# Output steps token tile by token tile, two product banks that swap by group, and QKV weights without a gap, in a fused attention and feed-forward kernel

## The chip, the cores and the metric

The kernel runs on one core of a Trainium2 chip. The metric is device time in microseconds, the median of the timed runs. The engines are PE (TensorE: matmuls, PEld its weight loads), ACT (ScalarE), DVE (VectorE), POOL (GpSimd) and SP (SyncE, which issues most DMAs). Each works through its own instructions in the order in which the program gives them out.

## What is computed

The input `x` has 2048 tokens of width 576. The result is the input, plus a local attention, plus a feed-forward layer with ReLU, both on the normalised input.

```
xn  = layernorm(x)
q, k, v = split(xn @ wqkv)            # 32 heads of width 18
logits[s, w] = q[s] . k[s - 2 w] / sqrt(18),   w = 0 .. 7   (no key before token 0)
a   = softmax(logits) @ v[s - 2 w]
out = x + a @ wo + max(xn @ w1, 0) @ w2        # w1: 576 x 4608, w2: 4608 x 576
```

## The kernel before

All matmuls run in a reduced-precision fp32 form. Each operand is kept as a high part (a rounded copy, made by ACT) and a low part (the difference, made by DVE), and each product is the sum of three: high by high, high by low, low by high. `hi_lo` makes such a pair.

The tokens are treated in two passes (`ph`) of 1024 each, eight tiles of 128 tokens. The 4608 hidden columns are treated in 18 steps `n` of 256 columns. A **group** `g` is one step `n` for one half `h` of the pass, 512 tokens; there are 72 groups. `m = g // 2` counts the weight sets; set `m` lies in `BUF[m % 2]`, as eight slots (T1, B11, T2, B21, T3, B22, T4, RR) in a high and a low half.

**First products** (`xn @ w1`) of a group make four hidden tiles of 256 columns of tokens (`j` = 0, 1) by 128 hidden columns (`f` = 0, 1). From the third weight set on they use a Strassen-Winograd form with seven products, P1 to P7, in `pstep`. Each is six matmuls (`terms`), or eight with the remaining 64 rows (`rest`). They accumulate in three PSUM banks, `bk2`, `bkA` and `bk3`; partial sums are copied to `bkA` (after P1), SN5 (after P5) and SN2 (after P6). `h_parts` applies the ReLU and makes the high part (`hhi`, ACT) and the low part (`hlo`, DVE) of a hidden tile. The tile (j, f) = (0, 0) comes out of P2, (1, 1) out of P7 by an addition into SN5, (0, 1) out of P3 by an addition into SN2, and (1, 0) out of P4 directly from the bank. In the trace, P-steps are the PE rows `bk<-xs`, `bk<-xa` and `bkA<-xa` with `bk<-xr` or `bkA<-xr` for the remaining rows; the additions are `sn<-bk,sn`.

**Second products** (`h @ w2`) of group `g - 1` are spread between the seven products of group `g`. An output step (`o_step(g, j, idx, k)`) is six matmuls for one hidden tile (`idx`) and one token tile of 128 (`k` = 0, 1; rows `po<-w2t`). Token tile `k` accumulates in the bank pair `po[k]`. After the last step of a token tile, ACT copies the sum out (`x<-po`) and writes the next token tile's running sum into the bank (`po<-x`, the seed). `items` lists the hidden tiles of a group and, in some groups, attention output times `wo` (`("wo", u)`, for four groups `u` of heads, and `("wo", NU)` for what is left). `o_list` gives the order of the output steps.

**Attention.** Eight times, QKV tiles (`qkv_tile`, rows `pm<-wset,xa`) are computed between the products of two groups; their weights (`wq_make`, view `wqset`) lie in the buffer that the next weight set will use, and are loaded as its slots come free. The attention proper is a list of long DVE operations (`later`), taken up when DVE has nothing more urgent. Its output is turned through DRAM (`turned`) and loaded by `wo_h`.

**Order.** The whole program is put in order by hand. The class `Order` keeps a clock per engine from estimated durations. Each small ACT or DVE operation has a slack, which becomes its due time; among those that are ready, the earliest due goes first. `force` gives out whatever a PE step needs before it. `tick` counts the steps of a group, and `plan` (`at(g, idx, f)`) hangs other work on a tick: weight preparation (`set_make`; `fine` after a QKV stage, when parts are made one by one), `w2_make`, `wo_make`, `wo_h`, and copies of weights to a packed form in DRAM (`w1_keep`, `w2_keep`, `wq_keep`, `wo_keep`), which POOL issues. The order of a group before:

```
steps = ("P5", 0), ("P1", 0), ("P6", 0), ("P2", None), ("P7", 1), ("P3", 1), ("P4", None)
cnt = {"P5": l0 // 3, "P1": l0 - l0 // 3 - l0 // 4, "P6": l0 // 4, "P7": l1 // 2, "P3": l1 - l1 // 2}
```

The second entry is the `j` whose output steps follow; with four steps for each `j` these are one after P5, two after P1, one after P6, two after P7 and two after P3.

## Time and profile before

| | |
|---|---|
| median of three timed runs | 1185.26 us (1184.56 to 1187.47) |
| profiled execution | 1186.34 us |
| its span, first to last instruction | 1184.6 us |
| mean granted TensorE clock | 0.997 |
| PE busy | 1142.5 us, 8528 matmuls |
| PE weight loads busy | 1115.6 us |
| DVE busy | 824.2 us |
| ACT busy | 742.4 us |
| DMA | 115.60 MB, 98 GB/s |

In the rows of the profile, a line of the kernel is often that of a helper: L284 is every matmul, L278 every ACT copy, L281 every DVE difference or sum, L562 the low part of a hidden tile. They are told apart by the names `out<-in`. "Idle before" and the brackets in the order of time say how long an engine stood and what released it. Matmul ends are modelled, so one row can run past the start of the next.

### The profile page before, as it was taken

Reading aid. Unit: us, or ns where it says so; the run is one execution under the profiler, and the core shown is the slowest. Engines: PE = TensorE matmul, PEld = TensorE weight load, DVE = VectorE, ACT = ScalarE, POOL = GpSimd, SP = SyncE. Lnnn points to the kernel's source line nnn. Section 1 sums busy time; section 2 is a strip of 40 time slices with the busy share of each in tenths; the row PEclk is TensorE's granted clock in tenths of the full one; section 3 lists DMA queues with packets and bytes.
Section 4 is the critical chain, followed back from the end, with each engine's and each line's share of the span. In section 5 each row is a group of like instructions: output and inputs, shape, how many; then the busy total and the mean of one; then the engine's idle time right before and its main releaser. Section 6 shows DMA issues by size and latency. Waiting matters only on the chain.

```text
span 1184.6 us, 21915 instructions
## 1 busy us (share of the span) xinstructions
PE 1142.5 (96%) x8528; PEld 1115.6 (94%) x8528; DVE 824.2 (70%) x1533; ACT 742.4 (63%) x1658; POOL 64.4 (5%) x97
## 2 busy tenths in 40 slices
PE   6999999999998999999989999999999999999998
PEld 5899899999998999899989999999999999999997
DVE  7648979952988179964793399499916994399641
ACT  5558467655666477576685567477737665676663
POOL 2200200110011001000120000000000000000000
PEclk9999999999999999999999999999999999999999
DMA  6652541562245133333352212231323213221322
GB/s 200 199 160 68 158 105 54 168 172 78 74 151 166 37 96 111 102 90 111 101 189 66 78 52 59 54 95 53 91 45 93 65 53 72 86 58 57 80 68 90
DMA packets 133544, 115.60 MB, mean 98 GB/s; under 512 B 54128, under 2 KB 112240, under 8 KB 133120
## 3 DMA queue, kind: packets, MB, share of 16 engines
q1 hardware_dynamic: 128192, 85.00, 26.2%
q0 software_dynamic: 5104, 28.90, 7.7%
q8 instruction: 67, 1.10, 0.4%
q14 instruction: 37, 0.30, 0.1%
q10 hardware_dynamic: 144, 0.29, 0.1%
HBM read 96.01 MB, written 36.50 MB: 112 GB/s over the span
## 4 chain that ended last, share of the span: by engine, by line
PE 64%; DVE 20%; ACT 6%; issue 4%; DMA 4%; SPq 0%; POOL 0%; DVEq 0%; ACTq 0%; POOLq 0%
PE po L284 26%; PE bk L284 18%; PE pm L284 14%; PE bkA L284 5%; DVE wset L281 4%; DVE pr L885 3%; DVE hlo L562 2%; DVE ts L281 2%; DVE pr L878 2%; DMA olo<-turned 1%; DVE sn L281 1%; ACT x L278 1%; ACT po L278 1%; ACT wset L278 1%; DMA wset<-wqc 1%
## 5 line engine op out<-in xcount | busy, mean ns | idle before, releaser
L284 PE MATMUL po<-w2t,hhi 128*128 128x256 f32 (+1 forms) x2304 | 399.9, 295 | 10.1 <-ACT po L278 9.9
L284 PEld LDWEIGHTS po<-w2t,hhi 128*128 128x128 f32 x2304 | 332.5, 188 | 18.1 <-ACT po L278 16.4
L284 PE MATMUL po<-w2t,hlo 128*128 128x256 f32 (+1 forms) x1152 | 244.2, 293 | 0.0
L278 ACT ACTIVATE x<-po 128x576 f32<-128x576 f32 x286 | 182.7, 645 | 97.5 <-PE po L284 94.6
L284 PE MATMUL bk<-xs,wset 128*128 128x256 f32 x1632 | 232.9, 278 | 2.2 <-DVE sn L281 2.2
L284 PEld LDWEIGHTS bk<-xs,wset 128*128 128x128 f32 x1632 | 212.2, 188 | 3.0 <-DVE sn L281 2.6
L284 PEld LDWEIGHTS po<-w2t,hlo 128*128 128x128 f32 x1152 | 190.4, 188 | 0.0
L278 ACT ACTIVATE po<-x 128x576 f32<-128x576 f32 x286 | 186.9, 654 | 3.1
L284 PE MATMUL pm<-wset,xa 128*128 128x432 f32 x768 | 172.9, 360 | 2.7 <-ACT wset L278 1.6
L284 PEld LDWEIGHTS pm<-wset,xa 128*128 128x128 f32 x768 | 140.3, 188 | 10.2 <-ACT wset L278 2.3
L284 PE MATMUL bk<-xa,wset 128*128 128x256 f32 x924 | 136.1, 285 | 12.5 <-DVE hlo L562 9.1
L284 PEld LDWEIGHTS bk<-xa,wset 128*128 128x128 f32 x924 | 123.0, 192 | 18.8 <-DVE hlo L562 14.6
L281 DVE TENSOR_TENSOR sn<-bk,sn 128x256 f32<-128x256 f32 x136 | 56.9, 419 | 102.8 <-PE bk L284 102.6
L281 DVE TENSOR_TENSOR w2t<-w2t 128x576 fp32r<-128x576 f32 (+1 forms) x72 | 54.0, 750 | 69.2 <-ACT w2t L278 68.6
L278 ACT ACTIVATE hhi<-sn 128x256 fp32r<-128x256 f32 x136 | 56.4, 415 | 64.0 <-DVE sn L281 63.7
L278 ACT ACTIVATE kk<-pm 128x144 f32<-128x144 f32 (+1 forms) x68 | 21.0, 309 | 116.3 <-PE pm L284 114.7
L848 DVE TENSOR_TENSOR pr<-qo,kk 128x1152 f32<-128x1152 f32 x64 | 85.0, 1350 | 0.0
L878 DVE TENSOR_TENSOR pr<-lg,v 128x1152 f32<-128x1152 f32 x64 | 84.9, 1349 | 0.1
L851 DVE TENSOR_REDUCE lg<-pr 128x64 f32<-128x1152 f32 x64 | 84.7, 1344 | 0.0
L284 PE MATMUL bk<-xr,wset 128*128 128x256 f32 x426 | 83.5, 278 | 0.0
L281 DVE TENSOR_TENSOR wset<-wset 128x512 fp32r<-128x512 f32 (+2 forms) x120 | 71.1, 599 | 12.4 <-ACT wset L278 12.3
L562 DVE SCALAR_TENSOR_TENSOR hlo<-bk,hhi 128x256 fp32r<-128x256 f32 x77 | 32.2, 418 | 57.1 <-ACT hhi L278 57.0
(132 smaller groups left out, 1394.4 us busy)
## 6 DMA issues: line engine op xcount, KB each, us to landing
w2t<-w2c SPq DMA_DIRECT2D x70, 288.0 KB, 2.8
wset<-w1c SPq DMA_DIRECT2D x106, 128.0 KB, 2.4
w1c<-in_w POOLq DMA_DIRECT2D x18, 576.0 KB, 8.9
w2c<-in_w POOLq DMA_DIRECT2D x18, 576.0 KB, 9.2
wset<-wqc SPq DMA_DIRECT2D x28, 216.0 KB, 2.5
out<-x SPq DMA_DIRECT2D x16, 288.0 KB, 2.2
wset<-w1c SPq DMA_DIRECT2D x70, 64.0 KB, 2.3
ts<-w1c SPq DMA_DIRECT2D x34, 128.0 KB, 2.9
```

What stands on the lines that cost most here:

```text
L278: nc.scalar.activation(o, i, func)
L281: nc.vector.tensor_tensor(o, a, b, op=op)
L284: nc.tensor.matmul(o, l, r, start=start, stop=stop, skip_group_check=True)
L562: nc.vector.scalar_tensor_tensor(lo, src, 0.0, f32(hi), op0=ALU.max, op1=ALU.subtract)
L848: nc.vector.tensor_tensor(pr[i], q, window(k, i), op=ALU.mult)
L851: nc.vector.tensor_reduce(s["lg"][:, i], pr.pop(i).rearrange(heads, d=Dh), axis=AX.X, op=ALU.add)
L878: nc.vector.tensor_tensor(pr[i].rearrange(heads, d=Dh), e, window(v, i).rearrange(heads, d=Dh), op=ALU.mult)
L885: nc.vector.tensor_tensor(o, z[:, 0:n], z[:, n : 2 * n], op=ALU.add)
```

## The change

- **Bank swap and order.** `pstep` takes the bank names by the parity of the group: P1, P6, P7 and P4 use `n2`, P5 and P3 use `n3`, and the two swap `bk2` and `bk3` from group to group. P1 comes first and P5 second. Of four output steps for `j` = 0, two follow P1 and two follow P6; none follows P5.
- **Output steps.** In most groups all steps of token tile 0 come before those of token tile 1. In groups with the last `wo` items, the two hidden tiles are still taken in turn and only the `wo` items go tile by tile.
- **QKV weights.** `wqset` is one run of ten parts without the gap between high and low half. The first QKV tile of each stage is given out in five parts, each after its own weight block.
- **Due times and ticks.** Slacks of several ACT and DVE operations change; in the `fine` weight preparation B11 goes first; the last `wo` loads move by a tick; three copies in DRAM move from groups 4 and 5 to groups 8 and 14.

```diff
     def wqset(p):
-        return BUF[(p + 1) % 2][:, :, 0 : 5 * 3 * UD].rearrange("p e (t c) -> p e t c", t=5)
+        z = BUF[(p + 1) % 2].rearrange("p e c -> p (e c)")
+        return z[:, 0 : 10 * 3 * UD].rearrange("p (e t c) -> p e t c", e=2, t=5)
...
         if fine:
-            parts(T1, T1, 1, TS[:, 0:1], [c1], 3.3)
-            parts(RR, RR, 1, z[:, RR : RR + 1], [got[RR]], 4)
-            parts(B11, B11, 1, z[:, B11 : B11 + 1], [got[B11], c1], 5.2)
+            parts(B11, B11, 1, z[:, B11 : B11 + 1], [got[B11], c1], 3.3)
+            parts(T1, T1, 1, TS[:, 0:1], [c1], 4)
+            parts(RR, RR, 1, z[:, RR : RR + 1], [got[RR]], 4.5)
...
-            WQOK.setdefault(p, []).extend(hi_lo(w[:, 0, kt], w[:, 1, kt], z, 3 * UD, [*g, *free], 2.5))
+            WQOK[p, kt] = hi_lo(w[:, 0, kt], w[:, 1, kt], z, 3 * UD, [*g, *free], 2.5)
...
     def pstep(g, name):
-        b2, bA, b3 = (z[:, 0:TBN] for z in (bk2, bkA, bk3))
+        n2, n3 = ("bk2", "bk3") if g % 2 else ("bk3", "bk2")
+        b2, bA, b3 = (bank_of[z][:, 0:TBN] for z in (n2, "bkA", n3))
...
         elif name == "P1":
-            BANK["bk2"] = [act(lambda: copy(bA, b2), TBN, [t, *BANK["bkA"]], 0.4)]
+            BANK[n2] = [act(lambda: copy(bA, b2), TBN, [t, *BANK["bkA"]], 1.0)]
         elif name == "P6":
-            BANK["bk2"] = [act(lambda: copy(SN2, b2), TBN, [t, *SNF[2]], 0.8)]
+            BANK[n2] = [act(lambda: copy(SN2, b2), TBN, [t, *SNF[2]], 1.4)]
         elif name == "P3":
-            a = dve(lambda: sub(SN2, b3, SN2, ALU.add), TBN, [t], 1.0)
-            SNF[2] = h_parts((g, 0, 1), SN2, [a], 2.8)
+            a = dve(lambda: sub(SN2, b3, SN2, ALU.add), TBN, [t], 0.8)
+            SNF[2] = h_parts((g, 0, 1), SN2, [a], 1.8)
         elif name == "P4":
-            BANK["bk2"] = h_parts((g, 1, 0), b2, [t], 0.2)
+            BANK[n2] = h_parts((g, 1, 0), b2, [t], 0.7)
...
     def wo_h(g, u, j):
-            s = [send(lambda: nc.sync.dma_start(v(f32(lo)), OT[u, i : i + ni].rearrange("i c k -> c i k")), 128, turned[ph, u], 2.5)]
+            s = [send(lambda: nc.sync.dma_start(v(f32(lo)), OT[u, i : i + ni].rearrange("i c k -> c i k")), 128, turned[ph, u], 2.5 if u < NU - 1 else 1.2)]
...
     def o_step(g, j, idx, k):
-            e = act(lambda: copy(X[i], whole(k)), D, [t], 0.5 + 0.3 * k)
+            e = act(lambda: copy(X[i], whole(k)), D, [t], 1.0)
...
-            POF[k] = [act(lambda: copy(whole(k), X[i2]), D, [e, XLAST[i2]], 1.2 + k * (1.2 if j else 0.4))]
+            POF[k] = [act(lambda: copy(whole(k), X[i2]), D, [e, XLAST[i2]], 2.2)]
...
     def o_list(g):
-        if g == NG - 1:
+        if ("wo", NU) not in items(g, 0) or g == NG - 1:
             return [(g, j, idx, k) for j in range(2) for k in range(2) for idx in range(len(items(g, j)))]
-        return [(g, j, idx, k) for j in range(2) for idx in range(len(items(g, j))) for k in range(2)]
+        order = [(idx, k) for idx in range(2) for k in range(2)] + [(idx, k) for k in range(2) for idx in (2, 3)]
+        return [(g, j, *z) for j in range(2) for z in order]
...
     def qkv_tile(p, u, i):
-        def f():
-            for z, (l, b) in enumerate(lst):
-                mm(o, l, wq[:, b[0], b[1]], z == 0, z == len(lst) - 1)
-
-        t = pe(f, 14 * 0.196, [*WQOK[p], *XOK[h, j], *BANK["pm"]])
+        parts = [lst]
+        if i == 0:
+            parts = [[z for z in lst if z[1][1] == kt] for kt in range(KT + 1)]
+        after = [*XOK[h, j], *BANK["pm"]]
+        for y, part in enumerate(parts):
+            def f():
+                for z, (l, b) in enumerate(part):
+                    mm(o, l, wq[:, b[0], b[1]], y == z == 0, part is parts[-1] and z == len(part) - 1)
+
+            t = pe(f, len(part) * 0.196, after + (WQOK[p, y] if i == 0 else WQOK[p, KT]))
+            after = []
...
-    at(4, 4, wo_keep)
-    at(5, 4, w1_keep, 0)
-    at(5, 5, w2_keep, 0)
+    at(8, 4, wo_keep)
+    at(14, 4, w1_keep, 0)
+    at(14, 5, w2_keep, 0)
...
-                        when = (gg, 20 if h else 9), (gg + 1, 9)
+                        when = (gg, 21 if h else 9), (gg + 1, 10)
...
-    steps = ("P5", 0), ("P1", 0), ("P6", 0), ("P2", None), ("P7", 1), ("P3", 1), ("P4", None)
+    steps = ("P1", 0), ("P5", None), ("P6", 0), ("P2", None), ("P7", 1), ("P3", 1), ("P4", None)
...
-        cnt = {"P5": l0 // 3, "P1": l0 - l0 // 3 - l0 // 4, "P6": l0 // 4, "P7": l1 // 2, "P3": l1 - l1 // 2}
+        cnt = {"P1": l0 // 2, "P6": l0 - l0 // 2, "P7": l1 // 2, "P3": l1 - l1 // 2}
```

More of the change, by code (lines that the diff above doesn't have):

```diff
@@ L567, in h_parts, with terms @@
         return [a, b]
-    def terms(bank, ws, xs, start):
-        o = bank[:, 0:TBN]
+    def terms(o, ws, xs, start):
         for j, (wp, xp_) in enumerate(((0, 0), (0, 1), (1, 0))):
@@ L577, in rest @@
         for e in range(2):
-            mm(bank[:, 0:TBN], w[:, e, RR, f], xr, False, e == 1)
+            mm(bank, w[:, e, RR, f], xr, False, e == 1)
     def slot(m, s):
@@ L605, in f_ @@
                         cnt += 1
-            rest(bank, m, f, XR[h][:, j])
+            rest(bank[:, 0:TBN], m, f, XR[h][:, j])
         ok = SETOK[m]
@@ L640, in pstep @@
         elif name == "P7":
-            s5 = BANK["bk3"]
-            t = pe(lambda: terms(bk2, slot(m, T3), sform(h, S3), False), T6, [*ok[T3], *BANK["bk2"]])
+            s5 = BANK[n3]
+            t = pe(lambda: terms(b2, slot(m, T3), sform(h, S3), False), T6, [*ok[T3], *BANK[n2]])
             a = dve(lambda: sub(SN5, b2, SN5, ALU.add), TBN, [t, *s5], 2)
-            BANK["bk2"] = [a]
+            BANK[n2] = [a]
             SNF[5] = h_parts((g, 1, 1), SN5, [a], 5)
@@ L692, in wo_h @@
             s = [
-                send(lambda rows=rows: nc.sync.dma_start(v(f32(lo)[rows]), OTR[i : i + ni].rearrange("i c k -> c i k")), 64, turned[ph, u], 1.5)
+                send(lambda rows=rows: nc.sync.dma_start(v(f32(lo)[rows]), OTR[i : i + ni].rearrange("i c k -> c i k")), 64, turned[ph, u], 1.2)
                 for rows in (slice(0, DR), slice(DR, P))
@@ L1116, in tile_body @@
     w2_keep(1)
-    KFREE[0] = WQOK[0]
+    KFREE[0] = [a for kt in range(KT + 1) for a in WQOK[0, kt]]
     OFREE[0] = [*W2OK[0, 0], *W2OK[0, 1]]
```

32 lines of the change are left out of this document (16 added, 16 removed).

## The prediction

> **What bounds the kernel now.** I read the page first, then the list of what TensorE waited for, then busy time in windows, and last the order of time around two of the waits. From the page:
>
> ```profile
> span 1184.6 us, 21915 instructions
> ...
> PE 1142.5 (96%) x8528; PEld 1115.6 (94%) x8528; DVE 824.2 (70%) x1533; ACT 742.4 (63%) x1658; POOL 64.4 (5%) x97
> ```
>
> TensorE (PE) sets the time. The change neither adds nor removes a matmul, so it can only take away or add idle time on PE. The profiled execution took 1186.34 us, 1.7 us outside its span; the median of the three timed runs is 1185.26, 1.1 below it. I carry differences over unchanged.
>
> The body of the kernel, from the first group of seven products (93.34) to the start of the third group from the end (1124.56), has these waits of PE (us in total, times, longest):
>
> ```profile
> PE po L284 <- ACT po L278: 9.7, 18, 1.8
> PE bk L284 <- DVE hlo L562: 9.1, 23, 0.9
> PE bk L284 <- DVE sn L281: 2.2, 2, 1.7
> PE pm L345 <- ACT v L278: 1.1, 1, 1.1
> PE pm L284 <- ACT qo L278: 0.9, 1, 0.9
> PE pm L1024 <- ACT v L278: 0.7, 1, 0.7
> PE po L284 <- DVE ohi L281: 0.3, 1, 0.3
> PE pm L284 <- ACT wset L278: 0.3, 1, 0.3
> ```
>
> Two causes make 18.8 of 24.3 us, 77%: a token tile's output bank, which ACT must read out and seed again (po), and the low half of a hidden tile, which must leave its bank before P1 writes there (hlo). These idle times understate the loss. Busy time in windows: the whole body; a plain group that waits for nothing; the next, with one listed wait; a group with one `wo` item; a group with three QKV tiles:
>
> ```profile
> 93.34:1124.56 1031.22, 1006.65 (x7564) 985.17 (x7563) 748.38 (x1377) 659.11 (x1474) 49.23 (x67) 1.00 0.33 91
> 428.23:440.17 11.94, 11.94 (x100) 11.94 (x99) 10.77 (x18) 8.54 (x19) 0.00 (x0) 1.00 0.29 84
> 440.17:452.96 12.79, 12.46 (x100) 12.12 (x99) 12.31 (x18) 8.78 (x20) 0.00 (x0) 1.00 0.16 45
> 957.92:972.98 15.06, 15.06 (x124) 15.06 (x123) 15.06 (x30) 9.16 (x21) 0.64 (x1) 1.00 0.28 73
> 1011.42:1031.86 20.44, 20.44 (x142) 20.07 (x141) 7.15 (x19) 11.88 (x32) 0.00 (x0) 1.00 0.27 79
> ```
>
> (Columns after the length: PE, weight loads, DVE, ACT, POOL.) The clock is 1.00 throughout. The second plain group is 0.85 us longer than the first, though PE counts as idle in 0.33 of it: around each wait the pipelining of weight loads and matmuls breaks too. So I count the loss in two ways. First, a floor: 65 groups at 11.94 = 776.1; 56 QKV tiles at (20.44 - 11.94)/3 = 2.83, 158.7; 12 groups with one `wo` item at 15.06 - 11.94 = 3.12, 37.4; the two groups with both last `wo` items (6 + 4 matmuls where one item has 6) at 5.2, 10.4: 982.6 together, 48.6 below 1031.22, with 40 small transposes inside the 48.6. Second, weight loads idle: 1031.22 - 985.17 = 46.1, less 0.37 per three QKV tiles without any wait, 6.9: 39. I take 43 us, and 77% of it, 33 us, for the two causes.
>
> The matmul column alone gives 1031.22 - 1006.65 = 24.6, of which 77% is 19. The Trainium skill (Perfetto Trace Analysis, Identifying the Most-Contended Engine) says that matmul busy time is a bad measure of headroom because matmuls are pipelined, and that weight-load time is the better one. The trace bears it out in the 0.85 against 0.33 above; a forecast by the matmul column would save about a third less.
>
> **The change part by part.** Here is one such wait in order of time (start, length), a plain group's end and the next one's start:
>
> ```profile
> 1041.10 0.39 PE L284 MATMUL bk<-xr,wset 128*128 128x256 f32 x2
> 1041.33 0.68 PE L284 MATMUL po<-w2t,hhi 128*128 128x256 f32 x4
> ...
> 1042.11 0.68 PE L284 MATMUL po<-w2t,hhi 128*128 128x256 f32 x4
> 1042.19 0.42 DVE L281 TENSOR_TENSOR sn<-bk,sn 128x256 f32<-128x256 f32 x1
> ...
> 1042.89 0.85 PE L284 MATMUL bk<-xa,wset 128*128 128x256 f32 x6
> ...
> 1043.80 0.84 PE L284 MATMUL bk<-xs,wset 128*128 128x256 f32 x6
> ...
> 1044.44 1.35 DVE L848 TENSOR_TENSOR pr<-qo,kk 128x1152 f32<-128x1152 f32 x1
> ...
> 1044.65 0.38 ACT L278 ACTIVATE hhi<-bk 128x256 fp32r<-128x256 f32 x1
> 1044.79 0.79 PE L284 MATMUL po<-w2t,hhi 128*128 128x256 f32 x4
> 1044.92 0.42 ACT L278 ACTIVATE hhi<-sn 128x256 fp32r<-128x256 f32 x1
> ...
> 1045.23 0.66 ACT L278 ACTIVATE po<-x 128x576 f32<-128x576 f32 x1
> ...
> 1045.70 0.42 DVE L562 SCALAR_TENSOR_TENSOR hlo<-bk,hhi 128x256 fp32r<-128x256 f32 x1
> 1046.04 0.41 DVE L562 SCALAR_TENSOR_TENSOR hlo<-sn,hhi 128x256 fp32r<-128x256 f32 x1
> 1046.18 0.96 PE L284 MATMUL bk<-xa,wset 128*128 128x256 f32 x6 [0.35 <-DVE hlo L562]
> ```
>
> Start to start, a product of eight matmuls takes 0.91 (1042.89 to 1043.80), one of six therefore 0.68, an output step 0.78 (1041.33 to 1042.11).
>
> *Banks and order of the seven.* Before, P4's bank is written again by P1, with P5 and one output step between: 0.91 + 0.78 = 1.69 us after P4. ACT takes 0.38 for the high half; then the low half stands behind an attention operation of 1.35 on DVE and ends at 1046.12, too late. After, the banks swap: P1 takes the bank that P3 left (released by an addition, not by a pair of halves, with two output steps and P4 between as before), and P4's bank is next written by P5, after P1 and two output steps: 0.68 + 1.56 = 2.24. Each such wait gets 0.55 us. The 23 waits average 0.40 and the longest is 0.9, so nearly all vanish. In the same way P5 now lies between P1's copy and P6, which waits for it, and two output steps instead of one between P6's copy and P7.
>
> *Output steps token tile by token tile.* Before, a token tile's bank gets its last step third or fourth of four; from there to its next first step lie one output step and two products, 0.78 + 0.91 + 0.68 = 2.37, for a copy out and a seed (0.66, the copy alike: 1.3). After, tile 0 is finished by the second step and tile 1 by the fourth, and two steps and three or four products follow before the same bank is needed: at least 1.56 + 0.91 + 0.91 + 0.68 = 4.06. The extra 1.7 us cover all of the 18 waits but the longest. What remains is ACT standing at the head of its queue for a DMA:
>
> ```profile
> olo<-turned SPq DMA_DIRECT2D x30, 128.0 KB, 2.4
> ...
> 473.10 9.00 DMA olo<-turned
> ...
> 482.12 0.42 ACT L278 ACTIVATE ohi<-olo 128x256 fp32r<-128x256 f32 x1 [4.90 <-DMA olo<-turned]
> ...
> 484.12 0.80 PE L284 MATMUL po<-w2t,hhi 128*128 128x256 f32 x4 [1.79 <-ACT po L278]
> ```
>
> (From the page, the chain and the order of time.) This load usually lands in 2.4 us and took 9.00. ACT idled 4.90 for it, with the read-outs queued behind, and PE 1.79. Nothing in the change shortens that DMA, but tile 0's read-out and seed can now precede the waiting copy. I leave 5 us of the 33 for what remains of both causes: 28 gone.
>
> *The price of the new order.* The second output step of a group now needs the second hidden tile (from P3's sum) one step earlier. Before, two steps, P4, P5, a step, P1 and another step lie between P3 and that use; after, two steps, P4, P1 and a step. That is 2 x 0.78 + 0.91 + 0.68 + 0.78 = 3.93, less 0.16 by which the recorded end of 1041.49 overlaps the next start: 3.8. In the rows above the chain (addition, high half, low half) ends at 1046.45, 4.96 after P3, which would be 1.2 late. But the addition ended at 1042.61 and ACT took up the high half only at 1044.92, after work that the old due times put first. The change gives the chain earlier due times (0.8 and 1.8 for 1.0 and 2.8) and the read-out later ones (1.0 and 2.2). Addition, 0.42 and 0.41 without queueing end at about 2 us. Between no cost and the 41 us worked out under the rivals I take 5, near the short end, because this row's delay is queueing behind work that has just gained 1.7 us.
>
> *QKV weights.* The first QKV tile now takes the weights in five parts. Its listed waits on weights in the body are 0.3 us. At the start:
>
> ```profile
> 24.64 1.26 PE L284 MATMUL pm<-wset,xa 128*128 128x432 f32 x5 [1.26 <-ACT wset L278]
> ...
> 29.34 0.80 PE L345 MATMUL bk<-ident,pr 128*128 128x128 f32 x4 [2.22 <-DVE mv L316]
> ```
>
> Up to 1.26 could be filled, but PE then waits 2.22 for a normalisation that would end no sooner. I take 0. Without the gap, the low part of the third weight block no longer lies on B22's slot, so its load may start after P7 instead of P3; its high part still does, so 0 again. B11 before T1 in the weight preparation follows the new order: 0.
>
> *Copies in DRAM.* `wo` and the second pass's first `w1` and `w2` are copied four to nine groups later. They stay well ahead of their use, and POOL, SP and ACT keep their other orders except for the last `wo` loads, moved by a tick and with less margin. The moved copies can lengthen other loads: the bound is from 0 to two more collisions like the one above, 4 us. I take 0, since the copies leave the busy start as well. The Trainium skill (DMA: Bandwidth & Descriptors, Issuing engines are not separate DMA queues) says that transfers from all issuers interleave on the same engines; the 9.00 against 2.4 above agrees, and by that rule the moved copies cost something wherever a load meets them.
>
> The sum: -28 + 5 = -23 on the profiled time, 1186.3 - 23 = 1163.3; on the median, 1162.3.
>
> **The rivals.** *The second hidden tile comes late (slower).* If ACT and DVE keep the chain from P3 as late as now, it replaces the waits removed. Its first and last instance (end of P3's last matmul, end of the low half):
>
> ```profile
> 200.38 0.39 PE L284 MATMUL bk<-xr,wset 128*128 128x256 f32 x2
> ...
> 205.12 0.41 DVE L562 SCALAR_TENSOR_TENSOR hlo<-sn,hhi 128x256 fp32r<-128x256 f32 x1
> ...
> 1065.80 0.39 PE L284 MATMUL bk<-xr,wset 128*128 128x256 f32 x2
> ...
> 1071.54 1.18 DVE L562 SCALAR_TENSOR_TENSOR hlo<-sn,hhi 128x256 fp32r<-128x256 f32 x1
> ```
>
> These are 4.76 and 6.53 against 3.8, late by 1.0 and 2.7. Read so in every group, 22 would be late (groups with QKV tiles between excepted), 41 us in all. Then the time is 1185.3 - 28 + 41 = 1198. It is slower than before from about 28/41, two thirds of that lateness. Against it: the queueing just shown has slack to give.
>
> *DVE becomes the bound beside attention (smaller gain).* In 440.17:452.96 DVE is busy 12.31 of 12.79, so that group can lose 0.48 of its 0.85 unless attention spreads: 56%. The saving is then 13, and the time 1172. Against it: the group at 957.92 has DVE busy for all of its 15.06 and PE loses nothing, and in the QKV groups DVE works 7.15 of 20.44, so attention has room to run on.
>
> *Nothing changes.* ACT and DVE, whose order is written out by estimates, give the slack away again, and the time is 1185.
>
> **How the numbers follow.** The forecast has 0.58, its own range 1151 (all 33 go, and 1 more) to 1169 (the new wait and moved copies cost 7 more). The DVE case has 0.22, 1169 to 1181. No change has 0.06, and slower 0.14, with 1198 as its centre and 1189 as its near end. About 0.3%, 3.6 us, is what a measurement here can tell from nothing. So faster 0.80, same 0.06, slower 0.14. The range is 1150 to 1186: the slower case and a small tail below are left out.
>
> **What would show it.** Right: the two top causes among PE's waits fall from 18.8 us to below 5, the plain group with attention is near 11.94 instead of 12.79, and weight loads idle about 23 us less. The steps fail if output steps wait for the low half from P3's sum (po waiting for hlo), if po still waits for ACT for more than 5 us, or if a group's DVE is full while PE waits for it. The forecast as a whole is wrong if body and end keep their lengths, or if the seven-product groups without attention grow beyond 11.94.

## The result, and the profile after

The changed kernel takes 1172.28 us (1168.43 to 1173.23) where the kernel before, run beside it, takes 1185.45 (1184.56 to 1187.47): a ratio of 0.9881, 95% interval 0.9854 to 0.9907. It is faster by 13 us; the forecast was 1162.3, a gain of 23. The profiled execution took 1173.04. From its page:

```profile
span 1171.2 us, 21895 instructions
...
PE 1135.0 (97%) x8528; PEld 1115.0 (95%) x8528; DVE 819.2 (70%) x1533; ACT 754.1 (64%) x1658; POOL 63.4 (5%) x97
```

The matmuls are the same 8528. The lines of the kernel have moved by one for PE, ACT and the differences (L285, L279, L282), the low part of a hidden tile is L563. What PE waited for in the body, now 94.17 to 1113.00 (us in total, times, longest):

```profile
PE bk L285 <- DVE hlo L563: 8.5, 15, 1.0
PE bk L285 <- DVE sn L282: 2.8, 3, 2.3
PE po L285 <- ACT po L279: 2.4, 4, 0.9
PE pm L346 <- DVE pr L335: 2.0, 1, 2.0
PE po L285 <- DVE ohi L282: 1.4, 1, 1.4
PE pm L1032 <- ACT v L279: 1.3, 1, 1.3
PE pm L285 <- DVE wset L282: 0.8, 2, 0.5
PE po L285 <- DVE hlo L563: 0.7, 1, 0.7
```

One of the two top causes is nearly gone (po for ACT, 9.7 to 2.4), the other is almost as large as before (bk for hlo, 9.1 to 8.5), though it strikes less often. Busy time in windows, with the columns of the prediction: the body, the plain attention group that took 12.79 before, a group that begins its attention's products with V, and a QKV group.

```profile
94.17:1113.00 1018.83, 998.74 (x7564) 983.67 (x7563) 745.93 (x1377) 670.80 (x1476) 49.82 (x70) 1.00 0.33 95
437.23:449.16 11.93, 11.93 (x101) 11.93 (x99) 11.05 (x16) 9.38 (x21) 0.00 (x0) 1.00 0.20 65
945.75:961.92 16.17, 15.49 (x124) 15.13 (x123) 16.02 (x33) 9.86 (x21) 0.64 (x1) 1.00 0.19 52
1001.09:1021.40 20.31, 20.31 (x143) 19.95 (x141) 7.12 (x19) 12.10 (x33) 0.00 (x0) 1.00 0.25 71
```

The body is 12.4 us shorter, the end after it 1.8 shorter, and the body begins 0.8 later: 13.4, the difference of the spans. Group by group (from the start of a first product to the next group's), the body lost 21.7 us in some groups and gained 9.3 in others (groups are counted from 0; the body is groups 4 to 68). So the question is what made some groups longer: the groups at 945.75 and 1072.39 (58 and 66) took 15.06 before and now 16.17; groups 21 and 22 together 43.4 where 41.9 stood; and the groups in which the second pass's input is normalised (33 to 37) 86.8 for 83.8.

### The profile page after: what moved, and what is told of

It reads as the page before. It is cut to its first block, busy times and chain, and to the rows that moved or that the text cites. A ratio compares the mean times of both kernels' runs of the same rounds, so it can differ in the third digit from the quotient of the medians.

```text
span 1171.2 us, 21895 instructions
## 1 busy us (share of the span) xinstructions
PE 1135.0 (97%) x8528; PEld 1115.0 (95%) x8528; DVE 819.2 (70%) x1533; ACT 754.1 (64%) x1658; POOL 63.4 (5%) x97
## 4 chain that ended last, share of the span: by engine, by line
PE 69%; DVE 19%; DMA 5%; ACT 4%; issue 3%; POOL 0%; SPq 0%; POOLq 0%; DVEq 0%; ACTq 0%
PE po L285 29%; PE bk L285 20%; PE pm L285 15%; PE bkA L285 4%; DVE pr L886 2%; DVE hlo L563 2%; DVE wset L282 2%; DVE pr L893 2%; DVE lg L859 2%; DMA olo<-turned 2%; DVE ts L282 1%; DVE pr L856 1%; DMA wset<-w1c 1%; ACT po L279 1%; DVE sn L282 1%
## 5 line engine op out<-in xcount | busy, mean ns | idle before, releaser
L285 PE MATMUL po<-w2t,hhi 128*128 128x256 f32 (+1 forms) x2304 | 397.2, 294 | 2.4 <-ACT po L279 2.4
L285 PEld LDWEIGHTS po<-w2t,hhi 128*128 128x128 f32 x2304 | 335.9, 188 | 4.5 <-ACT po L279 3.6
L279 ACT ACTIVATE x<-po 128x576 f32<-128x576 f32 x286 | 185.6, 649 | 147.5 <-PE po L285 144.0
L285 PE MATMUL po<-w2t,hlo 128*128 128x256 f32 (+1 forms) x1152 | 244.6, 293 | 0.7 <-DVE hlo L563 0.7
L285 PE MATMUL bk<-xs,wset 128*128 128x256 f32 x1632 | 234.4, 279 | 8.5 <-DVE hlo L563 8.5
L285 PEld LDWEIGHTS bk<-xs,wset 128*128 128x128 f32 x1632 | 212.0, 189 | 12.7 <-DVE hlo L563 12.2
L285 PEld LDWEIGHTS po<-w2t,hlo 128*128 128x128 f32 x1152 | 190.7, 188 | 0.9 <-DVE hlo L563 0.9
L279 ACT ACTIVATE po<-x 128x576 f32<-128x576 f32 x286 | 186.9, 654 | 6.2
L285 PE MATMUL pm<-wset,xa 128*128 128x432 f32 x768 | 171.8, 360 | 1.1 <-DVE wset L282 0.9
L285 PEld LDWEIGHTS pm<-wset,xa 128*128 128x128 f32 x768 | 140.5, 188 | 8.5 <-DVE wset L282 1.9
L285 PE MATMUL bk<-xa,wset 128*128 128x256 f32 x924 | 132.6, 281 | 7.0 <-ACT xa L279 4.0
L285 PEld LDWEIGHTS bk<-xa,wset 128*128 128x128 f32 x924 | 120.8, 191 | 8.4 <-ACT xa L279 4.3
L282 DVE TENSOR_TENSOR sn<-bk,sn 128x256 f32<-128x256 f32 x136 | 57.3, 421 | 97.7 <-PE bk L285 55.5
L279 ACT ACTIVATE kk<-pm 128x144 f32<-128x144 f32 (+1 forms) x68 | 21.1, 310 | 121.8 <-PE pm L285 120.0
L282 DVE TENSOR_TENSOR w2t<-w2t 128x576 fp32r<-128x576 f32 (+1 forms) x72 | 53.9, 748 | 64.2 <-ACT w2t L279 63.8
L279 ACT ACTIVATE hhi<-sn 128x256 fp32r<-128x256 f32 x136 | 56.1, 413 | 46.7 <-DVE sn L282 45.5
L886 DVE TENSOR_TENSOR pr<-lg,v 128x1152 f32<-128x1152 f32 x64 | 85.1, 1352 | 0.1
L856 DVE TENSOR_TENSOR pr<-qo,kk 128x1152 f32<-128x1152 f32 x64 | 84.6, 1350 | 0.0
L285 PE MATMUL bk<-xr,wset 128*128 128x256 f32 x426 | 83.7, 278 | 0.0
L282 DVE TENSOR_TENSOR wset<-wset 128x512 fp32r<-128x512 f32 (+2 forms) x120 | 71.5, 600 | 12.7 <-ACT wset L279 12.4
L279 ACT ACTIVATE wset<-wset 128x512 fp32r<-128x512 f32 (+2 forms) x120 | 65.4, 550 | 10.4 <-DMA wset<-wqc 8.3
```

Source lines behind the costliest of these rows:

```text
L279: nc.scalar.activation(o, i, func)
L282: nc.vector.tensor_tensor(o, a, b, op=op)
L285: nc.tensor.matmul(o, l, r, start=start, stop=stop, skip_group_check=True)
L856: nc.vector.tensor_tensor(pr[i], q, window(k, i), op=ALU.mult)
L886: nc.vector.tensor_tensor(pr[i].rearrange(heads, d=Dh), e, window(v, i).rearrange(heads, d=Dh), op=ALU.mult)
```

## Experiments

Each is the changed kernel with the edits named at it, timed in turn with the kernel before on the same chip. The ratio is to the kernel before (its medians were 1185.1 to 1185.9).

| run | median us | ratio | 95% interval |
|---|---|---|---|
| changed kernel | 1172.28 | 0.9881 | 0.9854 to 0.9907 |
| e3_no_swap | 1192.43 | 1.0055 | 1.0039 to 1.0070 |
| e4_no_tiles | 1214.37 | 1.0244 | 1.0225 to 1.0262 |
| e11_both_undone | 1187.98 | 1.0018 | 1.0005 to 1.0032 |
| e8_p3_old | 1172.58 | 0.9889 | 0.9871 to 0.9908 |
| e6_no_qkv | 1174.58 | 0.9905 | 0.9889 to 0.9920 |
| e7_old_copies | 1170.92 | 0.9876 | 0.9857 to 0.9895 |
| e2_p4_due | 1172.97 | 0.9899 | 0.9879 to 0.9919 |
| e1_softmax_cost | 1177.50 | 0.9925 | 0.9909 to 0.9941 |
| e5_slack8 | 1169.21 | 0.9866 | 0.9845 to 0.9887 |
| e9_act_copies | 1170.27 | 0.9866 | 0.9847 to 0.9885 |
| e10_costs_copies | 1162.86 | 0.9787 | 0.9765 to 0.9810 |
| e12_first_copies_back | 1157.39 | 0.9759 | 0.9743 to 0.9775 |

### The two main parts, each alone

**e3_no_swap** undoes the swap and the order of the seven (and what follows them: due times of the steps, the place of B11); the tile order stays.

```diff
-        n2, n3 = ("bk2", "bk3") if g % 2 else ("bk3", "bk2")
-        b2, bA, b3 = (bank_of[z][:, 0:TBN] for z in (n2, "bkA", n3))
+        b2, bA, b3 = (z[:, 0:TBN] for z in (bk2, bkA, bk3))
...
-    steps = ("P1", 0), ("P5", None), ("P6", 0), ("P2", None), ("P7", 1), ("P3", 1), ("P4", None)
+    steps = ("P5", 0), ("P1", 0), ("P6", 0), ("P2", None), ("P7", 1), ("P3", 1), ("P4", None)
...
```

> The changed kernel with the bank swap, the order of the seven products, their due times and the order of the first weight parts as before; output steps still go token tile by token tile. If the two parts do what the forecast says of each, P1's waits for the low half come back (9.1 us listed before, about 16 us with the restarts) and P5's (8.5 listed) go: 1175 to 1180. If the order of output steps makes nearly all of the gain: 1170 to 1174. If the swap does: 1183 or more.

**e4_no_tiles** undoes the tile order and the due times of the read-outs; the swap stays.

```diff
...
-        if ("wo", NU) not in items(g, 0) or g == NG - 1:
+        if g == NG - 1:
             return [(g, j, idx, k) for j in range(2) for k in range(2) for idx in range(len(items(g, j)))]
-        order = [(idx, k) for idx in range(2) for k in range(2)] + [(idx, k) for k in range(2) for idx in (2, 3)]
-        return [(g, j, *z) for j in range(2) for z in order]
+        return [(g, j, idx, k) for j in range(2) for idx in range(len(items(g, j))) for k in range(2)]
```

> The changed kernel with output steps in the old order (the two token tiles by turns) and the due times of read-out and seed as before; bank swap and new order of the seven stay. If the two parts do what the forecast says of each, po waits for ACT come back (9.7 us listed in the body before, about 17 with restarts): 1184 to 1190. Rival: the swap alone gives most of the gain, 1172 to 1177. A second rival: with two output steps after P1 and none after P5, the old order of output steps leaves a seed even less time than before, and the time is above 1190, slower than the kernel before.

**e11_both_undone** makes both edits.

> The changed kernel with both main parts undone (second products product by product, first products in the old order on fixed banks); left of the change are the layout of wqkv's parts, the QKV stage's first tile by parts, and the moved copies. Each main part alone was slower than the kernel before: tiles alone 1.0055, swap alone 1.0244. Theory (each main part raises the wait that the other takes away, and the small parts are worth 0 to 3 us, by the run without QKV parts 2.3): 1180 to 1186 us, ratio 0.996 to 1.001, waits of po for ACT and bk for hlo as in the kernel before, about 10 and 9 us. Rival (the small parts carry a good share of the gain): under 1178 us.

The top waits of PE in the body, first of e3, then of e4, then of e11:

```profile
PE bk L285 <- DVE hlo L563: 21.4, 26, 2.3
...
PE po L285 <- ACT po L279: 1.5, 2, 0.9
```

```profile
PE po L285 <- ACT po L279: 22.4, 43, 1.8
PE bk L285 <- DVE sn L282: 8.5, 3, 5.3
PE bk L285 <- DVE hlo L563: 2.7, 4, 1.0
```

```profile
PE po L285 <- ACT po L279: 10.7, 19, 1.6
PE bk L285 <- DVE hlo L563: 8.4, 21, 0.9
```

Each main part takes away its own wait and raises the other: with the tile order alone, po for ACT falls to 1.5 and bk for hlo rises to 21.4; with the swap alone it is the other way round, 2.7 and 22.4. Alone, each makes the kernel slower than before; together they make it faster. Of the expectations, e3 lies far above the 1175 to 1180 us of its first case; its last case, "1183 or more", has the number but not the reason, since the swap by itself is slower still. In e4 the second rival held. Not all of e4's 24.7 us in the body (1055.9 for 1031.2) are waits of po: groups 13 and 14 alone are 9.0 us longer, 5.28 of it one wait of PE (the longest for sn above) behind a weight load for which ACT stood 9.15 us. With both undone the waits are those of the kernel before and the time is 0.2% above it, 2 us above the range that was expected, so the small parts alone bring nothing. The swap and the new order of the seven were not tried apart.

### The terms that the prediction set at nothing, and the new price

**e8_p3_old** puts the due times behind P3 back.

```diff
-            a = dve(lambda: sub(SN2, b3, SN2, ALU.add), TBN, [t], 0.8)
+            a = dve(lambda: sub(SN2, b3, SN2, ALU.add), TBN, [t], 1.0)
...
-            SNF[2] = h_parts((g, 0, 1), SN2, [a], 1.8)
+            SNF[2] = h_parts((g, 0, 1), SN2, [a], 2.8)
```

> The changed kernel with the due times of the chain behind the sixth first product back at 1.0 (sum) and 2.8 (its halves), where the change has 0.8 and 1.8. With these the second hidden tile's low half is laid up to 1 us later, while the second products now ask for that tile earlier than before. Theory (the prediction's rival of the late second hidden tile was kept off by these due times): second products wait for hlo in 10 groups or more, 0.3 to 1.0 us each, where the changed kernel has one such wait of 0.7 us: 1176 to 1184 us. Rival (the tile is early enough by the place of the second products alone): that wait stays under 2 us in all and the time is 1170 to 1175.

The rival of that expectation held: po waits for hlo once, 0.7 us, and the time does not move. The second hidden tile was not saved by its due times. What left it room, the places of the output steps or the later due times of the read-out, was not tried alone.

**e6_no_qkv** lays `wqset` with its gap again and lets a QKV stage's first tile wait for all parts.

```diff
-        return z[:, 0 : 10 * 3 * UD].rearrange("p (e t c) -> p e t c", e=2, t=5)
+        return BUF[(p + 1) % 2][:, :, 0 : 5 * 3 * UD].rearrange("p e (t c) -> p e t c", t=5)
...
+        t = pe(f, 14 * 0.196, [*WQOK[p], *XOK[h, j], *BANK["pm"]])
```

> The changed kernel with wqkv's halves laid with a gap again and each QKV stage's first tile waiting for all five parts of its weights at once, as in the kernel before. Theory of the prediction (the parts lie off the path, priced at 0): 1171 to 1174 us, and the wait of the first QKV tile for its last weights not over 1 us longer than in the changed kernel at each of the 8 stages. Rival (the order of the other work hangs on it: a QKV tile that can begin with its first part lets the groups behind begin earlier, 8 stages by about 1 us): 1177 to 1182 us, with a longer wait for wset's or wqkv's sums (VectorE's) at the stages' first tiles.

The median is 2.3 us above the changed kernel's, and the intervals overlap. Of the groups with QKV tiles one is longer, group 6 (27.4 to 29.0, with a wait of 1.1 us for ACT's `qo`); the others differ by 0.3 us or less. The time lies between the ranges of the theory and of the rival. So a worth of some 2 us fits, and 0 is not excluded.

**e7_old_copies** moves the three DRAM copies back.

```diff
-    at(8, 4, wo_keep)
-    at(14, 4, w1_keep, 0)
-    at(14, 5, w2_keep, 0)
+    at(4, 4, wo_keep)
+    at(5, 4, w1_keep, 0)
+    at(5, 5, w2_keep, 0)
```

> The changed kernel with the three copies of split weights to DRAM at their old places (groups 4 and 5 in place of 8 and 14). Theory of the prediction (their move costs and brings nothing): 1170 to 1175 us, same groups up to 0.3 us each but for groups 4 to 15. Rival (the late copies stand in the way of loads of groups 14 to 21, where three waits of 1.3 to 2.3 us lie behind a late transfer): 1167 to 1170, those waits gone.

The move brings nothing that can be measured. The waits behind late transfers stayed (ACT 3.3 us at 342.3 and 4.1 at 371.9), so these three copies are not their cause.

### The wait for hlo that stayed

It is P5 now that waits, for the bank that P4 filled one group earlier. The order of time at 1072, start of a group in which the products with V begin:

```profile
1072.16 0.39 PE L285 MATMUL bk<-xr,wset 128*128 128x256 f32 x2
...
1073.45 0.37 ACT L279 ACTIVATE hhi<-bk 128x256 fp32r<-128x256 f32 x1
...
1073.69 2.15 DVE L893 TENSOR_TENSOR pr<-pr 128x576 f32<-128x576 f32 x4
...
1075.77 0.42 DVE L563 SCALAR_TENSOR_TENSOR hlo<-bk,hhi 128x256 fp32r<-128x256 f32 x1
...
1076.24 0.97 PE L285 MATMUL bk<-xs,wset 128*128 128x256 f32 x6 [0.67 <-DVE hlo L563]
```

P4 ends at 1072.55 and the low half at 1076.19, 3.64 later. In the kernel before, the same group had it 1.68 after P4:

```profile
1084.74 0.39 PE L284 MATMUL bk<-xr,wset 128*128 128x256 f32 x2
...
1085.45 0.38 ACT L278 ACTIVATE hhi<-bk 128x256 fp32r<-128x256 f32 x1
...
1086.40 0.41 DVE L562 SCALAR_TENSOR_TENSOR hlo<-bk,hhi 128x256 fp32r<-128x256 f32 x1
```

Of the 1.96 us of difference 0.57 arise on ACT (the high half is ready 1.27 after P4, at 1073.82, where it was ready 0.70 after) and the rest on DVE, which had begun four attention additions at 1073.69. Why would an order that knows what is due put 2.15 us of attention there? Either the due time is too late (0.7 us after P4, 0.2 before), or the order's clock for DVE is wrong at that point. The code's estimates have one candidate: an operation of n elements is taken as n/960 + 0.062 us, so a softmax reduction over 512 as 0.595 and the reciprocal of 64 as 0.129. Groups of instructions by line (count, busy us, mean ns):

```profile
L875 DVE TENSOR_REDUCE r<-lg 128x64 f32<-128x512 f32 x8 | 9.2, 1154 | 1.8 <-ACT lg L872 1.8
L868 DVE TENSOR_REDUCE m<-lg 128x64 f32<-128x512 f32 x8 | 9.2, 1150 | 7.5 <-POOL lg L862 7.5
...
L878 DVE RECIPROCAL r<-r 128x64 f32<-128x64 f32 x8 | 4.4, 545 | 0.1
```

Together 1.5 us more per softmax than the order believes. The same estimates stand in the kernel before, where this group had no such wait; they do harm here together with the new order.

**e2_p4_due** tests the first answer.

```diff
-            BANK[n2] = h_parts((g, 1, 0), b2, [t], 0.7)
+            BANK[n2] = h_parts((g, 1, 0), b2, [t], 0.2)
```

> The changed kernel, with P4's halves given their old due time (0.2 instead of 0.7), and nothing else. Rival (due time): P5's waits for the low half fall from 8.5 us to below 3 and the time to 1164 to 1167. Theory (late DVE): the due time decides only between operations that are ready together, and in the estimated order this low half was never late; time within 1.5 us of 1172 and the groups at 945.8 and 1072.4 still at 16.2.

The time did not move, and the group at issue (66) took 16.15 for 16.17. It is not the due time.

**e1_softmax_cost** tests the second: the order gets the measured lengths.

```diff
-        a = add(sm_max, n, [z])
+        a = add(sm_max, 1040, [z])
...
-        a = add(sm_sum, n, [a])
-        add(sm_rcp, 64)
+        a = add(sm_sum, 1040, [a])
+        add(sm_rcp, 460)
```

> The changed kernel, with three estimates of the softmax corrected in the program's own ordering (its two reductions count 1040 elements instead of 512, the reciprocal 460 instead of 64); no instruction is added or removed. Theory (late DVE): P5's new waits for the low half of P4's tile (15 waits, 8.5 us listed) come from DVE standing about 1.8 us behind its estimated order from each softmax on, because the two reductions take 1.15 us where the order counts 0.595 and the reciprocal 0.54 where it counts 0.13. Then the groups after a softmax that took 16.2 us (at 945.8 and 1072.4) fall to 15.2, these waits fall below 3 us, and the time falls by 5 to 8 us to 1164 to 1167. Rival (due time): the waits come from the later due time of P4's halves (0.7 for 0.2); then nothing changes here, 1171 to 1174.

The group that stands at 945.75 in the changed kernel (58), in this run:

```profile
954.54:969.60 15.06, 15.06 (x125) 15.06 (x123) 15.06 (x31) 9.72 (x20) 0.64 (x1) 1.00 0.20 57
```

15.06 in place of 16.17, with DVE busy throughout and PE waiting for nothing. Groups 11, 12, 44, 50, 59, 66 and 67 shrank as well, by 0.5 to 1.3 us each; 15 waits of 8.5 us became 5 of 5.7. The cause is shown for these groups. The waits that are left, 5.7 us, are above the 3 that were expected, and the time was not as expected: it rose to 1177.5. The loss is mainly in groups 14 (29.2 to 35.4), 20 (16.5 to 19.6) and 35 (18.0 to 20.3). Group 14, in order of time and in windows:

```profile
254.09 0.29 ACT L279 ACTIVATE v<-pm 128x144 f32<-128x144 f32 x1 [4.61 <-DVE pr L886]
...
254.62 3.25 PE L285 MATMUL pm<-wset,xa 128*128 128x432 f32 x8 [3.86 <-ACT qo L279]
```

```profile
250.00:258.00 8.00, 4.14 (x15) 3.70 (x14) 6.13 (x11) 0.47 (x2) 3.75 (x6) 0.67 0.19 60
258.00:266.00 8.00, 8.00 (x48) 7.75 (x47) 2.89 (x13) 3.34 (x10) 0.51 (x2) 0.91 1.03 308
```

A QKV tile overwrites the V buffer that the attention's last product with V (L886) still reads. The order has no such dependency in its estimates: ACT stood 4.61 us at the head of its queue, PE 3.86, and the granted clock was low from 252.67 to 259.49, as the rows of both windows show (third number from the end). In the whole body this trace has 27.3 us at half clock and the changed kernel's has 6.8. At half the clock work takes about twice its time (in e5 six matmuls took 1.60 us for 0.84), so by estimate up to 10 us more are lost this way, and the body is 6.7 us longer (1025.56). So what took the gain back is the clock as much as the waits themselves.

**e5_slack8** adds to e1 one number, by which attention work is let in a little more often ahead of something more urgent.

```diff
-    SLACK = 0.6
+    SLACK = 0.8
```

> The changed kernel with the softmax reductions at their measured length (1.14 us each, reciprocal 0.54) in the order's estimates, as in the run e1_softmax_cost, and besides with the order's slack 0.6 -> 0.8, by which the order lays the last product with V of the second attention task (its V buffer is overwritten by the next QKV tile) some 6 us ahead of that tile again. Nothing of the arithmetic changes. Theory (the 5.2 us that e1 lost against the sum came from order slips that it knows nothing of: the V buffer's 4.6 us in group 14 and what the granted clock made of it): group 14 goes back from 35.4 to about 29.2, the groups 58, 66, 59, 67, 11, 12, 44, 50 stay short as in e1, and the time is 1163 to 1169 us, 3 to 9 under the changed kernel. Rival (any other order of these instructions strikes some wait of its own of 2 to 5 us, the hidden-tile wait being only the one that happened in this order): new waits over 2 us in other groups, and 1171 to 1179.

Group 14 came back to 29.0, and the groups behind the softmax stayed short. But groups 20 to 22 took 63.4 us (59.9 in the changed kernel), 28 took 17.4 (16.4), 35 20.0 (18.0). The median, 1169.2, is at the edge of the theory's range and its interval overlaps the changed kernel's: no gain shown by this alone.

### The transfers that come late

In groups 20 to 22 and 28, ACT stands at the head of its queue for a transfer. What it waited for between 340 and 500 in the changed kernel, and in order of time the longest of these waits with PE behind it:

```profile
ACT ohi L279 <- DMA olo<-turned: 4.4, 2, 2.3
ACT wset L279 <- DMA wset<-wqc: 4.0, 2, 3.4
```

```profile
374.57 0.56 ACT L279 ACTIVATE wset<-wset 128x432 fp32r<-128x432 f32 x1 [3.43 <-DMA wset<-wqc]
...
376.53 0.96 PE L285 MATMUL bk<-xa,wset 128*128 128x256 f32 x6 [2.26 <-DVE sn L282]
```

Between the two rows DVE stood 3.15 us for the low half of that weight, and the addition `sn` that PE waits for came behind it, at 376.06. Why the load is late can be read from POOL's own order of time, whose queue issues the copies of weights to DRAM:

```profile
360.96 0.94 POOL L794 MEMSET v<- 1x1008 f32 x1 [23.03 <-ACT po L279]
361.86 0.65 POOL L407 DMA_DIRECT2D w1c<-in_w  x1
...
364.75 0.50 POOL L410 DMA_DIRECT2D w2c<-in_w  x1
```

The copies are meant to go out one pair in two groups. POOL stood 23 us before the attention's clearing of `v`, and behind it three pairs, 576 KB each copy, went out in 3 us (the first and the last are shown). The transfers of this stretch (330 to 380), KB each and median us to landing:

```profile
wset<-wqc SPq DMA_DIRECT2D x4, 216.0 KB, 8.2
...
olo<-turned SPq DMA_DIRECT2D x2, 128.0 KB, 5.4
```

**e9_act_copies** lets ACT issue these copies, at the same places of the written order.

```diff
-        kept["w1", n] = o_.keep(lambda: nc.gpsimd.dma_start(W1C[n], w1[:, 2 * n * P : 2 * (n + 1) * P]), 590)
+        kept["w1", n] = o_.keep(lambda: nc.scalar.dma_start(W1C[n], w1[:, 2 * n * P : 2 * (n + 1) * P]), 590)
...
```

> The changed kernel with the copies of split weights to DRAM started from ScalarE's instruction stream in place of GpSimd's; their places in the written order stay, nothing else changes. In the changed kernel they start in clumps, since GpSimd stands before them at the attention's masks: none between 336.5 and 361.9, then six of 590 KB within 2.9 us, and the loads issued behind them land after 8 to 9 us where others take 2 to 3. Theory (ScalarE's waits of 2.3, 3.4 and 2.1 us for a transfer at 345.6, 374.6 and 476.6, and the TensorE waits behind them, come from these clumps): those loads land in under 5 us, groups 20 to 22 take 56.5 us together in place of 59.9 and group 28 15.1 in place of 16.4; the time falls by 3 to 6 us, to 1166 to 1169. Rival (the transfers are late by the amount of traffic alone, however it is spread, or the issue on ScalarE costs as much as it saves): the three waits stay within 1 us of their lengths or move to other groups, 1171 to 1175.

In the same stretch of this run:

```profile
wset<-wqc SPq DMA_DIRECT2D x4, 216.0 KB, 2.6
olo<-turned SPq DMA_DIRECT2D x3, 128.0 KB, 3.2
```

None of ACT's waits for a transfer is left between 340 and 500; groups 20 to 22 take 55.0 us in place of 59.9, group 28 16.1 in place of 16.4 (it waits for hlo there), the body 1014.4 in place of 1018.8. But the body begins 3.7 us later, since the seven copies that POOL had sent off between 39 and 44 us now go out between 76 and 113, five of them by 91, into the loads of groups 2 to 4, and group 4 takes 14.1 for 11.9:

```profile
97.83 0.62 PE L285 MATMUL bk<-xa,wset 128*128 128x256 f32 x3 [1.99 <-ACT wset L279]
```

So the theory holds for the waits; the time, 1170.3, is 1.3 us above its range and not told apart from the changed kernel's. The kind of queue changes with the issuer too, but the first pair of POOL's clump landed in 4.5 and 5.8 us, and a pair of ACT's at the same place of e10 (362.1) in 4.6 and 5.6; the clump's last pair took 10.9 and 11.8. So I put it down to the clump, not to the kind of queue. The Trainium skill (DMA: Bandwidth & Descriptors, Issuing engines are not separate DMA queues) has it that transfers run on the same 16 DMA engines whichever engine started them, and that starting them from several engines saves only the time of starting. No run here measures that by itself; the gain in e9 is in when the copies start, with loads of 216 KB landing after 2.6 us in place of 8.2.

**e10_costs_copies** makes the edits of e5 and of e9.

> The run e5_slack8 (softmax reductions at their measured length, slack 0.8) with ScalarE starting the copies as in e9_act_copies. In e5 the waits for a transfer were longer than in the changed kernel (3.6 at 344.8, 4.5 at 376.3, 3.1 at 479.0) and took back what the shorter groups behind the softmax gave (groups 20 to 22 and 28 took 63.4 and 17.5 against 59.9 and 16.4). Theory: both gains add up, since they lie in other groups; 1160 to 1165. Rival (another order finds another wait): 1166 to 1171.

1162.86, ratio 0.9787: a gain of 9 on the changed kernel, where each alone brought 2 to 3 by the medians. Groups 20 to 22 take 53.6 and 28 15.1. So the gains add up once the transfers are on time: e5's waits for them had been longer than the changed kernel's (4.5 us at 376.3).

**e12_first_copies_back** gives the first nine copies back to POOL.

```diff
-        kept["w1", n] = o_.keep(lambda: nc.scalar.dma_start(W1C[n], w1[:, 2 * n * P : 2 * (n + 1) * P]), 590)
+        kept["w1", n] = o_.keep(lambda: (nc.gpsimd if n in (1, 2, 3, 4) else nc.scalar).dma_start(W1C[n], w1[:, 2 * n * P : 2 * (n + 1) * P]), 590)
...
```

> The run e10_costs_copies with the first nine copies (the pairs of the first four later weight blocks and the second head's wqkv) started by GpSimd again; in the changed kernel these start between 1.5 and 43.6, ahead of everything they could disturb, while in e9 and e10 seven of them came between 76 and 111, among the loads of groups 2 to 4, and group 4's first product began 3.5 us later than in the changed kernel (97.9 against 94.2) and group 4 took 12.4 in place of 11.9. Theory: that is the whole loss at the start, so group 4 begins at 93 to 95 again and the rest keeps e10's lengths; 1157 to 1161 us. Rival (the start is late for another reason, or the traffic at 40 us then finds other loads late): 1161 to 1166.

1157.39, ratio 0.9759: faster than both kernels, 15 us below the changed one. The body begins at 92.9 and takes 1004.5. Its longest waits:

```profile
PE pm L346 <- DVE pr L335: 2.4, 1, 2.4
PE bk L285 <- DVE hlo L563: 1.7, 2, 1.0
PE po L285 <- DVE ohi L282: 1.4, 1, 1.4
```

What is left lies nearly all in groups 33 to 37, which take 88.9 us here, 86.8 in the changed kernel and 83.8 before: 18.8 of the 21.9 us above the prediction's floor of 982.6 (88.9 less three groups at 11.94 and two at 17.14; the 40 small transposes are among them). Why they grew was not tried, but the traces show part of it. Group 37 takes 15.95 in the changed kernel and 14.35 in e2 and e6, with the same two waits of PE (1.0 and 0.7 us): in the first the granted clock was halved for 3.41 us, in the other two it was not. In e12 groups 35 and 37 each have such a stretch. In group 35 of the changed kernel PE's listed waits are 3.3 us for 2.1 before, 2.0 of them for the normalised input (`pr` of L335), which it did not wait for before. Why that comes later stays open.

## Why the prediction was right, and where its steps were wrong

The direction and the range held; the size was 10 us too good. The range of 36 us is wide, and 1172.28 lies outside the forecast's own part of it, 1151 to 1169, in the part that the prediction gave to the case of DVE with a chance of 0.22. By its steps:

- **PE sets the time, and only its idle time can change.** Right. By the prediction's second measure, weight loads idle, the loss in the body fell from 46.1 to 35.2 us (1018.83 less 983.67): 11, where 23 was forecast. The first signal, that the two causes fall below 5 us, failed: they stand at 10.9. The plain attention group came down to 11.93, as forecast.
- **Tile by tile: the extra 1.7 us cover nearly all waits of po for ACT.** Right: 9.7 to 2.4, and e4 brings them back (22.4). That the order without it would be worse than before was not foreseen.
- **The swap: 0.55 us more, so nearly all waits for hlo vanish.** The mechanism is right (without the swap and its order 21.4, e3); the step that failed is the second half, "so nearly all vanish": 8.5 us stayed. It let the low half end where it ended before. In the group behind a softmax that was looked at it ended 2 us later after P4, 3.64 for 1.68. e1 shows why for eight groups: DVE runs behind the written order by what its reductions take over their estimate.
- **28 of 33 us gone, 5 new.** By groups 21.7 gone and 9.3 new. The new price was looked for in the wrong place: the second hidden tile costs 0.7, not 5, and not because of its due times, as the prediction argued (e8). The late low half of P4's tile, the late transfers and a halved clock are where the new loss was found.
- **5 us left over for ACT standing before a DMA.** The prediction saw the collision and took it as given. It could be had by itself: groups 20 to 22 alone are 4.8 us shorter without it (e9).
- **QKV parts, moved copies: 0.** The copies' 0 is shown within about 2 us (e7). The QKV parts are worth some 2 us, or nothing (e6). B11's place was not tried alone.
- **The rival "DVE becomes the bound", 1172.** The number came out by luck, the reason did not. The plain attention group has DVE busy 11.05 of 11.93 and loses nothing. Where DVE was full and PE waited (16.02 of 16.17), e1 made the group 1.1 us shorter with the same DVE work: not its capacity, but the place of one short operation in its queue. (It is the group that the prediction named, at 957.92 before, as one where PE loses nothing beside a full DVE.)
- **The rival of the late second hidden tile** did not come: one wait of 0.7 us. What raises the time above the kernel before is one main part without the other, which the prediction did not consider.
- **The clock as 1.00 throughout.** So it was in the body before. In the changed kernel it was halved for two stretches of 3.41 us, one of which made group 37 1.6 us longer than the same group of e2.

## What to carry to other kernels

Where two waits share the same slack, undo and try the cures together as well as alone: here each alone made the kernel slower and both made it faster. In a program whose order comes from estimated durations, hold the estimates of all long operations against the trace's means before tuning due times; a reduction estimated at half its length put a 0.4 us operation behind 2 us of others. And look at what else stands in the queue that issues background copies: if it waits for anything, the copies come in clumps.

## What was not expected of the hardware

**Waits much shorter than 3.4 us can halve the granted clock.** After the stand of 2.26 us at 376.53, and after the two waits of 0.7 and 1.0 us in group 37, PE's granted clock was halved for 3.41 us; after a wait of 2.05 us at 594.91 it was not (the clock is the third number from the end; the first row holds most of the first wait, the third row the wait at 594.91, the fourth the two of group 37):

```profile
374.73:378.14 3.41, 1.10 (x7) 0.90 (x8) 2.59 (x5) 2.80 (x6) 0.00 (x0) 1.00 0.68 227
378.14:381.56 3.42, 3.42 (x14) 3.16 (x15) 3.23 (x13) 2.74 (x7) 0.00 (x0) 0.50 0.24 34
...
593.19:596.60 3.41, 1.69 (x14) 1.72 (x15) 2.35 (x5) 2.44 (x4) 0.94 (x2) 1.00 0.53 172
613.67:617.08 3.41, 1.69 (x11) 1.22 (x11) 2.92 (x7) 3.03 (x7) 2.82 (x4) 1.00 0.92 295
617.08:620.49 3.41, 3.41 (x17) 3.41 (x16) 0.00 (x0) 0.77 (x2) 0.05 (x1) 0.50 0.34 101
```

So the length of one wait does not decide it. In all fourteen traces the half-clock stretches of the body, 27 of them, begin a whole number of windows of 3.413 us after the first clock record and last one or two windows. Sorted by the share of such a window at full clock in which PE is busy: all 15 windows under 0.44 (the first row has 0.32) were followed by half the clock, 12 of the 18 between 0.44 and 0.50 (the third and fourth rows), and none of the over 4000 with 0.53 or more. So in these traces it counts how much PE idles within one window, and a wait that a window's edge divides can pass without harm, as the same two waits did in e2 and e6. Near one half the traces leave it open, since matmul ends are modelled. Such a stretch costs up to 1.7 us, and whether a wait of this size brings one depends in part on luck. In e5 a wait of 2.15 was followed by six matmuls in 1.60 us, which take 0.84 at full clock. So part of what the late transfers cost is this.

The Trainium skill (TensorE: Matmul & The Clock Gate, Part 1: The HAM clock gate) gives about 3.4 us of idleness as what halves the clock. e4's stand of 5.28 us agrees with that: a window in which PE was busy for 0.04 of the time lies almost wholly inside it. The 2.26 here is shorter, and e1's clock fell at 252.67, 1.9 us into its stand of 3.86, so the measurement decides. The stretch at half clock, 378.14 to 381.56 by these rows, is about as long as the page's window of 3.4 us.

**One reduction runs at half the rate of another.** The softmax's reductions take 1.15 us over 512 elements of each partition, read in runs of 8 with a stride of 8. The reduction behind the products of q and k reads 1152 elements that lie side by side, in runs of 18, in 1.34, as long as a product of that size (1.35 at L856). An addition that writes 576 takes 0.75:

```profile
L859 DVE TENSOR_REDUCE lg<-pr 128x64 f32<-128x1152 f32 x64 | 84.2, 1344 | 0.0
...
L893 DVE TENSOR_TENSOR pr<-pr 128x576 f32<-128x576 f32 x64 | 46.1, 751 | 0.0
```

The order's estimates are 0.595, 1.262 and 0.662. So it is not reducing as such that is slow here; whether the stride or the short runs make it so was not tried.
